# Outputs of paired chunks written channel-major by 64x32 tiles, in a fused gated linear attention and cosine-gated MLP on one core

## The chip, the core and the metric

The kernel runs on 1 core of one Trainium2 chip. The metric is the device time of one execution in microseconds. A run of before takes 192.56 us in the median of 13 (191.68 to 193.63).

## The reference

Inputs are q, k, v and f_logit of shape (4 batches, 8 heads, 768 steps, 48 channels) in float32, w_in (384 x 2048) and w_out (2048 x 384).

```python
f = 1.0 / (1.0 + np.exp(-f_logit))
state = np.zeros((B, H, D, D))
for t in range(S):
    state = f[:, :, t, :, None] * state + np.einsum('bhd,bhe->bhde', k[:, :, t], v[:, :, t])
    y[:, :, t] = np.einsum('bhd,bhde->bhe', q[:, :, t], state)
x = y.transpose(0, 2, 1, 3).reshape(B * S, H * D)
h = x @ w_in
out = (h * np.cos(h)) @ w_out
```

So there is a linear attention with a decay per channel, and then a two-layer network ("moe" in the code) over 3072 tokens with h cos h between the layers.

## The kernel before

The sequence is cut into chunks of 128 steps, 24 in all (6 per batch). Within a chunk the recurrence becomes matrix products: q times the cumulated decay b, k divided by it (bi), scores k q, a causal mask, and masked scores times v; what came before the chunk enters as q times the state. The first 12 chunks are handled as six **pairs** (`attend2`), the other 12 as **single** chunks (`attend`). A pair puts neighbouring time steps into one SBUF partition, so chunk x of the pair (x = 0, 1) lies in rows 64x to 64x+63, with an index e (or t in the loops) for even and odd steps.

The steps of a pair, by the lines of the profile:

- loads of k, q, v, f_logit by SP (L446; L438 for single chunks, and L426 for the weights);
- decay: exponential and logarithm on ScalarE (L484, L496), cumulated sums on TensorE (L507 to L513; L516 and L519 for single chunks), two exponentials out of PSUM (L524) into `b` and `bi`;
- products q b and k bi into `qk` on GpSimd or VectorE (L585; L679 for single chunks), cast of v into `vb` (L590, recorded at L432);
- transposes of `qk` on TensorE (L604) and their copy `qkt` (L606, recorded at L460; late single chunks use a DMA transpose, L692);
- scores on 64x64 tiles of TensorE (L617), mask `am` on VectorE (L623);
- the chunks' contribution to the state (`ps`, L637), then `move_state`: `st` = ps + state on VectorE (L542), `sz` = st times decay on GpSimd, in two halves (L549; a batch's first on VectorE), one after the other for the two chunks;
- the output `y` (function `pey`): state part L657, 96 moving columns for a pair of heads, and attention part L664, 64x128 tiles with 48 moving columns; it comes out with time in the partitions;
- `finish`: copy to `yb` in bf16 (L561), three transposes per chunk (`trx`, L568), and the copy to `xT` with channels in the partitions (L571); all copies are recorded at L460.

A single chunk's output (`pex`, L752) is already channel-major: the stationary operand is a slice of 32 channels of v (or of the state), the moving one the 128 columns of masked scores (or of transposed q), on tiles of 128 rows and 32 columns, four side by side. A 32-channel slice crosses from one head of 48 channels to the next in one slice of three; for these a second operand `vz` holds the 16 channels of each head beside zeros (L685, its four buffers are cleared at L378).

The network: `h` (L776) multiplies three 128-row parts of `xT` by w_in, cosine on ScalarE (L783), product `gT` on VectorE (L786), `o` (L798) multiplies 16 parts by w_out, copy `ot`, store by SP (L807, L810). It runs in units of 128, 128 and then 256 tokens, and its matmuls fill TensorE between the steps of the attention.

No order is written by hand. A planner (`Plan.run`) places every step on an engine by estimated costs: among the steps that could start within WINDOW ns of the earliest it takes the one with the lowest priority number. The table `PR` gives priorities (by kind of step: at, dec, f, h, k, o, tq, v, weights and gates for the switch of ScalarE's tables), `PIN` ties single steps to an engine. PSUM is one set of eight banks, from which every step takes one or two. `FORM` is the planner's cost of a change of TensorE's tile form. What the planner makes of it is a fixed order on each engine; each engine then runs its list in that order and waits at its head.

Of the kernel before, what the change touches and what calls it, by code (L numbers as in the profile page):

```python
# [116 lines left out]
class Plan:  # L117
# [6 lines left out]
    WINDOW = 200.0  # L124
# [128 lines left out]
def apart(tc, o, base):  # L253
# [13 lines left out]
    if banks and len(others) == len(banks):  # L267
        for b in banks:
# [11 lines left out]
    "at": [10.34, 1.66, 15.33, 9.78, -55.16, -54.85, -53.46, -27.65, -51, -51.02, -29.98, -1.78, 9.47,  # L280
          -24.05, -17.51, 26.44, 19.26, 41.61, 64.33, 60.95, 72.47, 41.29, 57.83, 70.66],
    "dec": [-40.13, -18.23, -118.54, -46.76, -113.79, -51.74],
    "f": [-33.54, 19.93, -13.27, 40.85, 11.69, 33.17, 10.24, 7.48, 19.13, 35.33, 34.56, -8.91, 83.83, 25.67,
          43.19, 50.91, 46.16, 41.23, 43.7, 50.92, 53.89, 87.57, 91.31, 90.43],
    "h": [9.97, 25.95, -30.53, 3.01, 6.76, -14.75, 87.35, 2.76, 40.79, 71.4, 37.51, 78.01, 62.23],
    "k": [-19.36, -9.86, -11.55, -8.7, 12.98, 15.54, 17.61, 50.25, 24.91, 19.36, 19.87, 27.13, 50.07, 53.19,
          47.56, 36.04, 66.28, 20.81, 59.57, 55.65, 83.79, 62.58, 85.61, 102.11],
    "o": [6.66, -5.11, 50.87, 98.39, 32.17, 119.14, -26.88, 103.85, 90.57, 149.42, 116.19, 123.67, 209.71],
    "tq": [29.88, 23.18, 15.76, 18.41, 3.3, 16.21, -23.62, 32.95, 98.96, 101.92, 58.74, 71.6, 53.32, 59.07,
          54.45, 42.26, 37.42, 40.36, 46.15, 7.47, 36.37, 39.29, 24.36, 18.36],  # L290
    "v": [-13.3, 8.45, -11.68, 3.43, 13.02, 15.37, 13.49, 28.89, 25.51, 21.76, 19.22, 48.22, 37.19, 43.36,
          51.52, 29.6, 40.85, 47.99, 28.14, 17.21, 52.36, 64.87, 53.96, 38.6],
    "w_in": [-7.72, -4.28, -1.16, -0.96],
    "w_out": [9.87, 4.13, 4.15, 9.92],
    "wc": [-56.67, -4.8, -15.98, -36.98, -13.35, -114.12, -134.73, -136.33],
    "gate": [None, 8, 3, 13, 20, 23],
}
PIN = {1: "DVE", 3: "ACT", 5: "POOL", 7: "POOL", 9: "POOL", 11: "DVE", 13: "POOL", 34: "DVE", 37: "POOL", 43:
       "DVE", 53: "DVE", 55: "DVE", 71: "DVE", 85: "DVE", 106: "DVE", 107: "POOL", 108: "POOL", 110: "DVE", 125:
       "ACT", 127: "DVE", 130: "DVE", 151: "ACT", 169: "POOL", 170: "POOL", 173: "ACT", 175: "ACT", 179: "DVE",  # L300
       187: "ACT", 189: "DVE", 213: "ACT", 219: "DVE", 231: "DVE", 232: "DVE", 234: "POOL", 235: "DVE", 253:
       "ACT", 277: "DVE", 295: "DVE", 297: "POOL", 298: "POOL", 301: "DVE", 305: "DVE", 319: "ACT", 342: "ACT",
       348: "DVE", 362: "DVE", 363: "DVE", 364: "POOL", 370: "DVE", 378: "DVE", 425: "POOL", 434: "ACT", 440:
       "POOL", 441: "ACT", 450: "DVE", 477: "DVE", 492: "POOL", 493: "ACT", 502: "DVE", 508: "POOL", 539: "ACT",
       545: "DVE", 560: "POOL", 561: "POOL", 576: "POOL", 577: "ACT", 582: "ACT", 603: "DVE", 624: "ACT", 633:
       "ACT", 639: "ACT", 640: "ACT", 670: "ACT", 691: "POOL", 692: "ACT", 701: "DVE", 707: "POOL", 717: "DVE",
       738: "DVE", 769: "DVE", 775: "POOL", 778: "ACT", 782: "ACT", 809: "ACT", 815: "ACT"}


def build(nc, cpool, ppool, q, k, v, f_logit, moe_w_in, moe_w_out, out):  # L310
    B, H, S, D = 4, 8, 768, 48
    C = 128
# [35 lines left out]
    def slots(name, n, shape, dt=BF16, zero=None):  # L348
        aps = [tl(shape, dt, f"{name}_{i}") for i in range(n)]
        if zero is not None and nc is not None:  # L350
            for t in aps:
                zero(t)
        return Slots(aps, name)
# [22 lines left out]
    vbB = halves("vb", 3, HD, BF16)  # L376
    vbS, vb2S = Banks(vbB, 1, [5, 4, 3, 2, 1, 0], "vb"), Banks(vbB, 2, [0, 2, 4], "vb2")
    vzS = slots("vz", 4, [128, NP, 96], zero=lambda t: nc.gpsimd.memset(t, 0.0))  # L378
# [4 lines left out]
    ybS = slots("yb", 2, [128, d_model])  # L383
# [14 lines left out]
    HB = lambda a: a.rearrange("p (h d) -> p h d", d=D)  # L398
# [159 lines left out]
    def finish(n, y, ycut, prio):  # L558

        yb, x = Val(ybS), xT[n]  # L560
        P.op("yb", {"ACT": act(384), "DVE": dve(384)}, lambda e: cp(e, yb.ap, ycut()),  # L561
             reads=[y], writes=[yb], prio=prio)
        px = Val(p1S)
        pxv = lambda: px.ap[:, 0:KM * C // 2].bitcast(BF16).rearrange("p (a n) -> p a n", n=C)

        def trx(e):
            for m in range(KM):
                nc.tensor.transpose(out=pxv()[:, m, :], in_=yb.ap[:, m * 128:(m + 1) * 128],  # L568
                                    identity=ident)
        P.op("trx", {"PE": mm(128, 3)}, trx, reads=[yb], writes=[px], prio=prio)  # L570
        P.op("xe", {"DVE": dve(384, 0.52), "ACT": act(384)}, lambda e: cp(e, x.ap, pxv()),  # L571
             reads=[px], writes=[x], prio=prio)

    E = lambda e: nc.vector if e == "DVE" else nc.gpsimd

    def attend2(b, c, n, ld, bt, bi, prio):
# [6 lines left out]
        for i in range(2):  # L583
            for j, (src, dec) in enumerate(((qf, bt), (kf, bi))):
# [5 lines left out]
        P.op("vb", {"POOL": 1050.0, "ACT": act(768, "S"), "DVE": 900.0}, lambda e: cast(e, vb.ap, vf.ap),  # L590
             reads=[vf], writes=[vb], prio=prio)
        twin = lambda j, p, e: qkv()[:, j, e, 2 * p:2 * p + 2, :].rearrange("p h d -> p (h d)")
        vv = lambda: vb.ap.rearrange("p (h e d) -> p e h d", e=2, d=D)
# [58 lines left out]
        py = Val(scS)  # L652

        def pey(e):
            for x in range(2):
                for p in range(NP if S[x] is not None else 0):
                    nc.tensor.matmul(py.ap[:, 512 * x + 96 * p:512 * x + 96 * p + 96],  # L657
                                     lhsT=qkts[p // 2].ap[:, 2 * x + p % 2, :],
                                     rhs=S[x].ap[:, p].rearrange("p t n -> p (t n)"), start=(p == 0), stop=False)
            for h in range(H):  # L660
                for t in range(2):
                    for x in range(2):
                        o = 512 * x + h * D
                        nc.tensor.matmul(py.ap[:, o:o + D],  # L664
                                         lhsT=ams[h // 4].ap[rows[x], h % 2, h % 4 // 2 * 2 + t, :],
                                         rhs=vv()[rows[x], t, h, :],
                                         start=(S[x] is None and h == 0 and t == 0), stop=(h == H - 1 and t == 1))
        P.op("y", {"PE": 845.0 if S[0] is not None else 680.0}, pey,
             reads=ams + [vb] + qkts + [x for x in S if x is not None], writes=[py], prio=prio,
             form=("full", "64x128"))  # L670
        for x in range(2):
            finish(n + x, py, lambda x=x: py.ap[:, 512 * x:512 * x + d_model], prio)

    def attend(b, c, n, ld, bt, bi, i, prio):
# [3 lines left out]
        for j, (src, dec) in enumerate(((qf, bt), (kf, bi))):  # L678
# [3 lines left out]
        vz = Val(vzS)  # L682
        P.op("vb", {"POOL": 530.0, "ACT": act(384, "S")}, lambda e: cast(e, vb.ap, vf.ap),
             reads=[vf], writes=[vb], prio=prio)
        P.op("vz", {"POOL": 270.0, "ACT": act(128, "S")}, lambda e: cast(  # L685
            e, vz.ap.rearrange("p s (r d) -> p s r d", d=48)[:, :, :, 0:16], vf.ap.rearrange(
                "p (s j d) -> p s j d", s=NP, d=16)[:, :, 2:4, :]), reads=[vf], writes=[vz], prio=prio)
# [34 lines left out]
        if c < NCH - 1:  # L722
            ps = Val(p1S)

            def pes(e):
                for p in range(NP):
                    nc.tensor.matmul(ps.ap[:, p * 2 * D:(p + 1) * 2 * D], lhsT=pair(1, p),  # L727
                                     rhs=vb.ap[:, p * 2 * D:(p + 1) * 2 * D],
                                     start=(p == 0), stop=(p == NP - 1))
            P.op("ps", {"PE": mm(96, 4)}, pes,  # L730
                 reads=[qk, vb] + ([S_in] if S_in is not None else []), writes=[ps], prio=prio)
            move_state(b, c, (ps, bt), lambda: ps.ap[:, 0:HD].rearrange("p (a t n) -> p a t n", t=2, n=D),
                       lambda: bt.ap[:, i, HD:], prio)
# [3 lines left out]
        def pex(e):  # L737
            ws, head = [], lambda h: am.ap[:, h % 2, h // 2, :]
            if S_in is not None:
                ws = [(t, S_in.ap[:, t // 3].rearrange("p t n -> p (t n)")[:, t % 3 * 32:t % 3 * 32 + 32],  # L740
                       qkt.ap[:, t // 3, :]) for t in range(12)]
            for r in range(2):
                for t in range(12):
                    s, k = t // 3, t % 3
                    if k == 1:
                        ws.append((t, vz.ap[:, s, 32 * r:32 * r + 32], head(2 * s + r)))
                    elif r == 0:
                        ws.append((t, vb.ap[:, 32 * t:32 * t + 32], head(2 * s + k // 2)))
            seen = set()
            for i, (t, w, m) in enumerate(ws):  # L750
# [5 lines left out]
             reads=[am, vb, vz, qkt] + ([S_in] if S_in is not None else []), writes=[px], prio=prio,  # L756
# [148 lines left out]
```

## Time and profile before

| | |
|---|---|
| median of 13 runs | 192.56 us |
| profiled execution, its own time | 192.56 us |
| its span, first to last instruction | 190.8 us |
| TensorE busy | 176.2 us, 92% |
| VectorE busy | 131.5 us, 69% |
| ScalarE busy | 127.0 us, 67% |
| GpSimd busy | 70.6 us, 37% |
| moe matmuls, L776 and L798 | 67.9 and 67.9 us |
| output of pairs, L657, L664 and L568 | 3.0, 3.7 and 4.0 us |
| output of single chunks, L752 | 4.7 + 4.1 + 3.5 us |

Busy times are of one execution. [...]the busy time of a group is longer than what it takes from TensorE; what it takes is read in the timeline, from the start of one group to the start of the next. In a row of instructions stand the line, the engine and operation, what is written and read, the shapes, and then the time and what ended the idle time before.

### The profile page before, as it was taken

To read this page: it belongs to the slowest core of one execution; us is meant where nothing else is said; L and a number is where in the kernel's file an instruction comes from. 1 tells how busy PE (TensorE), PEld (TensorE's weight loads), DVE (VectorE), ACT (ScalarE), POOL (GpSimd) and SP (SyncE) were. 2 spreads that over 40 slices of the span, in tenths; PEclk is the share of its full clock that TensorE was granted. 3 is DMA by queue.
4 is the path that set the end of the run, shared out by engine and by line. 5 is a ranking of instruction groups with operands and counts; after the bars stand their busy time and mean duration, and the time that the engine had idled before them with its cause. 6 is when DMAs were issued, how large, how long until landed. Compare 5 with 4: busy or idle time off the path is not lost.

```text
span 190.8 us, 5431 instructions
## 1 busy us (share of the span) xinstructions
PE 176.2 (92%) x2276; PEld 131.4 (69%) x2276; DVE 131.5 (69%) x169; ACT 127.0 (67%) x162; POOL 70.6 (37%) x109
## 2 busy tenths in 40 slices
PE   0688998999999999997799999999999999999993
PEld 0556897666788766686675668866778768876562
DVE  5478889859797929885798167996388895981100
ACT  5553867995488997797679947799955515861121
POOL 8544276043621113436932577205960240000000
PEclk9999999999999999999999999999999999999999
DMA  5999999989899998987999989973591101011122
GB/s 151 266 266 381 383 372 318 243 218 245 211 236 235 220 200 168 206 179 162 227 184 158 228 190 204 189 166 52 145 81 34 45 3 41 0 44 74 50 86 84
DMA packets 94121, 33.13 MB, mean 174 GB/s; under 512 B 87312, under 2 KB 92560, under 8 KB 94096
## 3 DMA queue, kind: packets, MB, share of 16 engines
q1 hardware_dynamic: 94096, 32.78, 74.1%
q8 instruction: 18, 0.29, 0.6%
q14 instruction: 7, 0.06, 0.1%
HBM read 25.17 MB, written 4.72 MB: 157 GB/s over the span
## 4 chain that ended last, share of the span: by engine, by line
PE 70%; DMA 8%; DVE 5%; issue 5%; POOL 5%; ACT 4%; SPq 3%; POOLq 0%; DVEq 0%; ACTq 0%
PE ps L798 30%; PE ps L776 26%; DMA ld<-in_q_dram 8%; PE ps L752 2%; PE ps L604 2%; PE ps L714 2%; SPq L446 2%; POOL sz L549 1%; DVE qk L585 1%; DVE am L623 1%; DVE gT L786 1%; ACT bi L524 1%; POOL qk L585 1%; PE ps L727 1%; POOL w_in_bf L432 1%
## 5 line engine op out<-in xcount | busy, mean ns | idle before, releaser
L776 PE MATMUL ps<-xT,w_in_bf 128*128 128x256 bf16 (+1 forms) x624 | 67.9, 265 | 0.5 <-DVE gT L786 0.5
L798 PE MATMUL ps<-w_out_bf,gT 128*128 128x384 bf16 (+2 forms) x400 | 67.9, 320 | 0.4 <-DVE xT L460 0.4
L783 ACT ACTIVATE cosh<-ps,halfpi 128x1024 bf16<-128x1024 f32 x48 | 53.0, 1113 | 20.0 <-PE ps L776 19.6
L786 DVE TENSOR_TENSOR gT<-ps,cosh 128x1024 bf16<-128x1024 f32 x48 | 57.9, 1221 | 10.3 <-ACT cosh L783 9.0
L776 PEld LDWEIGHTS <-w_in_bf 128*128 128x128 bf16 x624 | 56.1, 98 | 8.4 <-issue 0.8
L798 PEld LDWEIGHTS <-gT 128*128 128x128 bf16 x400 | 36.6, 98 | 21.7 <-issue 0.4
L549 POOL TENSOR_TENSOR sz<-st,b 64x192 bf16<-64x192 f32 x32 | 16.6, 519 | 31.9 <-DVE st L542 29.0
L717 DVE TENSOR_TENSOR am<-ps,umask 128x1024 bf16<-128x1024 f32 x12 | 14.5, 1217 | 6.7 <-ACT bi L524 3.7
L460 DVE COPY ot<-ps 128x384 f32<-128x384 f32 x12 | 6.6, 553 | 16.6 <-PE ps L798 16.6
L460 ACT COPY ot<-ps 128x384 f32<-128x384 f32 (+2 forms) x13 | 5.8, 455 | 16.4 <-PE ps L798 16.3
L623 DVE TENSOR_TENSOR am<-ps,pmask 128x1024 bf16<-128x1024 f32 x12 | 14.4, 1220 | 2.3 <-PE ps L617 2.2
L679 POOL TENSOR_TENSOR qk<-ld,b 128x384 bf16<-128x384 f32 x12 | 12.0, 1002 | 9.9 <-PE ps L798 5.5
L484 ACT ACTIVATE f<-f 128x768 f32<-128x768 f32 (+1 forms) x14 | 10.5, 747 | 4.8 <-DMA f<-in_f_logit_dram 4.8
L432 POOL CAST vb<-ld 128x384 bf16<-128x384 f32 (+1 forms) x13 | 7.8, 603 | 13.5 <-DMA ld<-in_v_dram 10.1
L524 ACT ACTIVATE b<-ps 128x776 f32<-128x776 f32 (+1 forms) x14 | 10.1, 722 | 3.1 <-PE ps L513 1.8
L679 POOL TENSOR_TENSOR qk<-ld,bi 128x384 bf16<-128x384 f32 x12 | 11.9, 998 | 0.0
L496 ACT ACTIVATE sp<-f 128x768 bf16<-128x768 f32 (+1 forms) x14 | 10.5, 752 | 0.4
L604 PE MATMUL ps<-ident,qk 128*128 128x128 bf16 x96 | 8.7, 250 | 1.8 <-POOL qk L585 1.1
L524 ACT ACTIVATE bi<-ps 128x768 f32<-128x768 f32 (+1 forms) x14 | 10.0, 717 | 0.0
L507 PE MATMUL ps<-sp,incl 128*128 128x384 bf16 x12 | 4.5, 378 | 5.4 <-ACT sp L496 5.3
L585 POOL TENSOR_TENSOR qk<-ld,b 128x384 bf16<-128x384 f32 x4 | 4.9, 1233 | 12.3 <-ACT b L524 10.6
L542 DVE TENSOR_TENSOR st<-ps,sz 128x384 f32<-128x384 f32 x16 | 8.8, 551 | 0.3 <-issue 0.2
(78 smaller groups left out, 189.4 us busy)
## 6 DMA issues: line engine op xcount, KB each, us to landing
f<-in_f_logit_dram SPq DMA_DIRECT2D x16, 192.0 KB, 4.2
ld<-in_k_dram SPq DMA_DIRECT2D x16, 192.0 KB, 3.8
ld<-in_q_dram SPq DMA_DIRECT2D x16, 192.0 KB, 3.9
gT<-in_moe_w_in_dram SPq DMA_DIRECT2D x4, 768.0 KB, 8.8
gT<-in_moe_w_out_dram SPq DMA_DIRECT2D x4, 768.0 KB, 11.7
ld<-in_v_dram SPq DMA_DIRECT2D x6, 384.0 KB, 5.4
out_dram<-ot SPq DMA_DIRECT2D x24, 96.0 KB, 2.6
ld<-in_v_dram SPq DMA_DIRECT2D x12, 192.0 KB, 3.6
```

Of the source, the lines that this page charges most:

```text
L460: (nc.scalar.copy if e == "ACT" else nc.vector.tensor_copy)(out=o, in_=i_)
L484: first = P.op("exp", {"ACT": act(384 * w, "S")}, lambda e, s=s: nc.scalar.activation(out=flat(ft.ap[:, s]), in_=flat(ft.ap[:, s]), func=A ...
L524: nc.scalar.activation(out=out_.ap[:, s, :], in_=pc.ap.rearrange("p (m n) -> p m n", m=w)[:, :, 0:n], func=AF.Exp, scale=sign)
L549: eng().tensor_mul(out=like(S_out.ap, pv())[s, ..., r, :], in0=srcap()[s, ..., r, :], in1=d[..., None].broadcast_to(list(d.shape) + [D]))
L604: nc.tensor.transpose(out=o[:, j, :, p, x, :], in_=twin(j, 2 * i + p, x), identity=ident)
L623: P.op("am", {"DVE": dve(1024)}, lambda e, sc=sc, am=am: nc.vector.tensor_mul(out=am.ap.rearrange("p r a n -> p (r a n)").rearrange("p (a ...
L679: P.op("qk", {"POOL": 1020.0}, lambda e, j=j, src=src, dec=dec: E(e).tensor_mul(out=qkv()[:, j, :, 0:D], in0=HB(src.ap), in1=HB(dec.ap[:, ...
L717: P.op("am", {"DVE": dve(1024)}, lambda e: nc.vector.tensor_mul(out=am.ap.rearrange("p r a n -> p (r a) n"), in0=sc.ap.rearrange("p (a n) ...
L776: nc.tensor.matmul(ph.ap[:, g * T:(g + 1) * T], lhsT=w_in_bf[:, f0 // 512, m, f0 % 512:f0 % 512 + 128], rhs=x[:, m, :], start=(g % (G // 2 ...
L783: nc.scalar.activation(out=co.ap, in_=ph.ap, func=AF.Sin, bias=halfpi),
L786: P.op("g", {"DVE": dve(1024)}, lambda e, ph=ph, co=co, gv=gv: nc.vector.tensor_mul(out=gv.ap, in0=ph.ap.rearrange("p (g t) -> p g t", t=T ...
L798: nc.tensor.matmul(po.ap[:, 0:z - a], lhsT=gT.ap[:, j, i * C:(i + 1) * C], rhs=w_out_bf[:, j, a:z], start=(j == 0), stop=(j == KF - 1))
```

## The change

`attend2` now writes its outputs channel-major as `attend` does. The matmuls of `y` are issued in two steps, one for each half of the heads (i = 0, 1), each as soon as that half's masked scores exist. The state part uses tiles of 128 rows and 32 columns, the attention part tiles of 64 rows (the chunk x) and 32 columns; both chunks' results go to one PSUM bank each, and one copy to `xT` follows. `yb`, `trx` and `finish` are gone.

`vb` is padded to 64 columns a head, with zeros in the last 16, so that a slice of 32 channels that crosses heads is read as two overlapping windows of it; `vz` goes, in single chunks too. `vb` of a pair is written with e outermost. The planner's WINDOW goes from 200 to 120, and nearly every entry of `PR` and `PIN` has another value, so the order of all engines is another.

```diff
-    WINDOW = 200.0
+    WINDOW = 120.0
...
-    vbB = halves("vb", 3, HD, BF16)
+    vbB = halves("vb", 3, H * 64, BF16, zero=lambda t: nc.gpsimd.memset(
+        t.rearrange("p (a d) -> p a d", d=64)[:, :, D:64], 0.0))
-    vzS = slots("vz", 4, [128, NP, 96], zero=lambda t: nc.gpsimd.memset(t, 0.0))
-    ybS = slots("yb", 2, [128, d_model])
...
-        py = Val(scS)
-
-        def pey(e):
-            for x in range(2):
-                for p in range(NP if S[x] is not None else 0):
-                    nc.tensor.matmul(py.ap[:, 512 * x + 96 * p:512 * x + 96 * p + 96], ...
...
-        P.op("y", {"PE": 845.0 if S[0] is not None else 680.0}, pey,
+        pxs, seen = [Val(p1S), Val(p1S)], set()
+        for i in range(2):
+            def pey(e, i=i):
+                ws, last = [], {}
+                for x in range(2):
+                    if S[x] is not None:
+                        ws += [(x, t, columns(S[x], t), qkts[i].ap[:, 2 * x + t // 3 % 2, :])
+                               for t in range(6 * i, 6 * i + 6)]
+                for e in range(2):
+                    for k in range(2):
+                        for t in range(6 * i, 6 * i + 6):
+                            for h, w in slices(t)[k:k + 1]:
+                                ws += [(x, t, vb.ap[rows[x], 512 * e + w:512 * e + w + 32],
+                                        ams[i].ap[rows[x], h % 2, h % 4 // 2 * 2 + e, :]) for x in range(2)]
...
+                for m, (x, t, w, a) in enumerate(ws):
+                    j = t % 4
+                    nc.tensor.matmul(pxs[x].ap[32 * j:32 * j + 32, t // 4 * C:t // 4 * C + C], lhsT=w, rhs=a,
+                                     start=(x, j) not in seen, stop=(i == 1 and last[x, j] == m))
+                    seen.add((x, j))
+            k = sum(x is not None for x in S)
+            P.op("y", {"PE": 225.0 + (96.0 if k else 0.0) + 88.0 * k}, pey,
...
+                 form=("128x32" if k else "64x32", "64x32"))
         for x in range(2):
-            finish(n + x, py, lambda x=x: py.ap[:, 512 * x:512 * x + d_model], prio)
+            P.op("xe", {"DVE": dve(384), "ACT": act(384)}, lambda e, x=x: cp(
+                e, xT[n + x].ap, pxs[x].ap[:, 0:HD].rearrange("p (a n) -> p a n", n=C)),
+                reads=[pxs[x]], writes=[xT[n + x]], prio=prio)
+
+    def slices(t):
+
+        s, k = t // 3, t % 3
+        return [(2 * s + k // 2, 128 * s + 40 * k)] if k != 1 else [
+            (2 * s, 128 * s + 32), (2 * s + 1, 128 * s + 48)]
```

In the tables, for example, the priorities of v:

```diff
-    "v": [-13.3, 8.45, -11.68, 3.43, 13.02, 15.37, ...
+    "v": [-13.48, 17.98, -0.36, -1.26, 5.93, -16.14, ...
```

## The prediction

> **What bounds the kernel now.** I read the page first, then the program's order of instructions before and after (which tells what stands behind what on every queue), then TensorE's timeline where the changed step runs, and last the waits that stop TensorE.
>
> ```profile
> PE 176.2 (92%) x2276; PEld 131.4 (69%) x2276; DVE 131.5 (69%) x169; ACT 127.0 (67%) x162; POOL 70.6 (37%) x109
> PE   0688998999999999997799999999999999999993
> DMA  5999999989899998987999989973591101011122
> PE 70%; DMA 8%; DVE 5%; issue 5%; POOL 5%; ACT 4%; SPq 3%; POOLq 0%; DVEq 0%; ACTq 0%
> ```
>
> TensorE is busy in 92% of the span and is 70% of the chain that ended last. Its idle slices are the head and two places near 85 to 90 us. VectorE, ScalarE and GpSimd have room on the average, so work taken from them pays only where TensorE waits for it. DMA is full up to about 125 us: a better order of loads can help, more speed of an engine cannot hasten them.
>
> To see what TensorE could save I laid its instructions end to end at the paces of its own timeline: 56 ns for 128 moving columns (8 transposes in 0.46 us at 49.70), 0.109 us for 256 (24 in 2.62 us), 0.162 us for 384 (8 in 1.30 us), and 0.10 us for each change of tile form. That gives about 167 us of work. The rest of the 190.8 us span is some 13.7 us up to the first moe matmul (20.41 us less 6.7 us of such work: the inputs, the chain of the first pair, and matmuls that run at half pace at first), some 7 us of waits after it, and 3.1 us behind the last matmul.
>
> **The pair's output step, before.**
>
> ```profile
> 80.31 0.50 PE L657 MATMUL ps<-sz,qkt 128*128 128x96 bf16 x8
> 80.74 0.57 PE L664 MATMUL ps<-vb,am 64*128 64x48 bf16 x32
> 81.25 0.62 PE L604 MATMUL ps<-ident,qk 128*128 128x128 bf16 x8
> 81.97 0.33 PE L568 MATMUL ps<-ident,yb 128*128 128x128 bf16 x3
> 82.14 0.33 PE L516 MATMUL ps<-sp,umask 128*128 128x384 bf16 x1
> ...
> 111.07 0.35 PE L752 MATMUL ps<-qkt,sz 128*32 128x128 bf16 x12
> 111.25 0.22 PE L752 MATMUL ps<-am,vb 128*32 128x128 bf16 x1
> ...
> 111.58 0.66 PE L798 MATMUL ps<-w_out_bf,gT 128*128 128x384 bf16 x3
> ```
>
> The first column is the start: TensorE is occupied from one start to the next. State part and attention part take 0.94 us (80.31 to 81.25), three transposes 0.17 us, twice a pair: 1.27 us. Where only one chunk has a state behind it (pairs 0 and 3) 4 of the 8 state matmuls fall out: 1.10 us. The lower rows are the single chunks' step, already of the new kind: 12 matmuls on four column tiles in 0.18 us, so three rounds of four at 56 to 60 ns, all four columns at work at once.
>
> **The same step after.** Per half of the heads: 12 matmuls of 128x32 (6 with one state), then 32 of 64x32. The new code sends the first along columns 0,1,2,3,0,1,0,1,2,3,0,1; [...]a column takes one at a time, so column 0, used four times, makes four rounds of 56 ns (two with one state). The second run, in each of its two passes, goes 0,1,2,3,0,1,1,0 in both row halves: columns 0 and 1 come three times, six rounds in all, 334 ns, though 32 matmuls on eight tiles could fit in four rounds. A half is 10 rounds, 0.56 us, a pair 1.11 us; with changes of form (in, between, and out, five for the pair) at 0.10 us it is 1.6 us, against 1.27 us with the transposes that go. For one state: 16 rounds 0.89 + 0.5 = 1.4 us against 1.1 us. That is 4 x 0.34 + 2 x 0.29 = +1.9 us. In the new order other steps stand together more often: changes of form over the whole kernel rise from 79 to 92 by the two orders, 13 and not the 18 that six pairs alone add, so 0.5 us comes off. **TensorE's work: +1.4 us.** The change makes the bound engine's work longer.
>
> [...] The row is above: column tiles with all 128 rows start together, 12 in 0.18 us. [...]I price by columns and rows; eight tiles at once, though, no row shows. [...] The row puts 0.10 us on it (the 32 small matmuls above, 16 pairs at 25 ns in 0.51 us from start to start, leave that), and I charge it 13 times.
>
> Bounds of the unknown: a 64x32 matmul costs 10.4 ns on average by my six rounds, 7 ns if the array packs better (-1.3 us over 384), 14 ns if eight tiles run at the pace of four, as at 111.07 (+1.4 us). I take 10.4, from the same timeline's rule that a busy column waits.
>
> **What is taken off the other engines.** Twelve yb copies (8 on ScalarE at 478 ns, 4 on VectorE at 557: 6.1 us); twelve vz casts (7 x 304 + 5 x 293: 3.6 us); four vz memsets at 412 ns, against three vb memsets near the 338 ns of the like row. The xT copies of pairs become f32: VectorE 552 in place of 353 ns, +0.2 us each. Pair vb casts write strided: between 824 ns (flat) and 1168 (the strided product) on GpSimd. None of this is on the path by itself; TensorE hides it except at three places.
>
> **Place 1, the head.**
>
> ```profile
> 16.35 1.09 PE L568 MATMUL ps<-ident,yb 128*128 128x128 bf16 x6 [0.57 <-ACT yb L460]
> 17.24 1.91 PE L604 MATMUL ps<-ident,qk 128*128 128x128 bf16 x16
> 20.41 1.04 PE L776 MATMUL ps<-xT,w_in_bf 128*128 128x128 bf16 x12
> ```
>
> Before, TensorE waits for yb and for its second copy (at half pace: six transposes take 0.9 us). These go. I followed the new order through with the old durations: the first q/k products are moved (k of half 0 to GpSimd, q of both halves to VectorE, where the second waits for its load at 7.45), which brings the second transposes to 8.65, 0.2 us earlier; the first qkt copies move to ScalarE (1.0 in place of 0.69 us) and hold up the second decay, so its last exponential ends at 16.1 instead of 15.2; the masks end at 14.4 instead of 13.9; the output's second half runs 15.0 to 16.05; the next transposes 16.05 to 18.1 instead of 17.24 to 19.1; the scores end at 19.5, the first moe matmul follows. The weights are no hindrance: v of the second pair now stands behind the first two w_in loads on SP's queue, and w_in lands 1.5 us earlier than its 17.0. So 20.41 becomes about 19.5 with 6.7 us of work before it in both: **-0.9 us**, and I add 0.2 us for the last w_in, cast at once by VectorE (26.8 before). Ends: -0.2 if the half-pace stretch lasts as long[...].
>
> **Places 2 and 3, near 90 us.**
>
> ```profile
> 89.05 0.33 PE L657 MATMUL ps<-sz,qkt 128*128 128x96 bf16 x4 [0.99 <-POOL sz L549]
> 91.10 0.34 PE L568 MATMUL ps<-ident,yb 128*128 128x128 bf16 x3 [0.25 <-DVE yb L460]
> 92.92 0.34 PE L727 MATMUL ps<-vb,qk 128*128 128x96 bf16 x4 [0.82 <-POOL qk L679]
> ```
>
> The waits for yb (0.4 us here, 0.2 at 57.4) have no successor: the xT copy reads the result itself. The wait for sz: in the new order 30 instead of 24 moe matmuls stand between the pair's state step and its output, 0.65 us more cover; but GpSimd does four qk products of 1.0 us ahead of that sz, and both halves of the output now stand behind it. I count half, -0.6. The third wait came from a q that SP issued at 86.03 and that landed at 90.3; in the new order the k and q of the first two single chunks stand some 25 us earlier in SP's queue and their products ahead of that sz, so -0.9. **Sum -2.1 us.** Other waits (some 3 us in small pieces, 0.45 at 138.6 behind the table load) I leave as they are: with every priority replaced some will go and some will come.
>
> **Sum.** +1.4 - 1.1 - 2.1 = -1.8 us on the profiled 190.8 us span, 189.0 us. That execution's own time is 192.56 us, 1.8 us around the span, and equals the median of the runs shown; so 190.7 us. Runs spread over 1%; a difference of 0.3%, 0.6 us, is about the least that a measurement can tell from none.
>
> **The rivals.** (a) The waits only change places: the gains near 90 us come back elsewhere, since TensorE stands behind sz chains in every pair. Then +1.4 - 1.1 - 0.6 (yb) = -0.3, 192.3 us, and a little worse order makes it slower; for it speaks that all queues are rearranged, against it the third wait's load, which is plainly earlier. (b) The eight tiles don't run at once: the place is the 64x32 run of each half, 384 matmuls; from 15 ns each (10.4 + 1.8 us / 384) the gain is used up; at 28 ns, two at a time, the time is 190.7 + 6.8 = 197.5 us. Against it the 64x64 rows, where four tiles in both directions share 32 matmuls in 0.57 us; for it that nothing here shows more than four. (c) The denser head reaches full pace sooner: 1.4 us more gained, 189.3. (d) The change doesn't earn it: order tables, pins and window are replaced too, so a gain may be the rearranged loads' alone; by my sum it is, but for the yb waits and the head's.
>
> **How the numbers follow.** Forecast 0.50, (c) 0.18, (a) 0.22, (b) 0.10. Of (a) 0.06 is faster, 0.08 the same, 0.08 slower; of the forecast 0.46 is faster, 0.04 the same; (b) is slower. Faster 0.70, same 0.12, slower 0.18. The range takes (c) with the better packing, -1.4 - 1.3, down to 188.0, and (a) with the 14 ns price, up to 193.7; most of (b) is left out.
>
> **What would show it.** Right: y of a half taking about 0.75 us from start to start with six steps of 56 ns in its 64x32 run; first moe matmul near 19.5; no matmul waiting for a q near 90 us; TensorE's matmuls up from 2276 to 2512 while its idle time falls by some 3 us. Wrong: 64x32 matmuls 14 ns or more apart; idle time before the output's first matmuls, by sz or am; a first moe matmul after 20.4.

## The result, and the profile after

The changed kernel takes 191.06 us in the median of 11 runs, before 192.95 in 48 runs taken beside it: ratio 0.989, 95% interval 0.9864 to 0.9917. Two of the 11 runs took 194.3 and 194.4 us, at a granted clock of 0.99, and are left out of the ratio. The profiled execution took 191.32 us with a span of 189.5, against 192.56 and 190.8.

From the page of after:

```profile
PE 176.6 (93%) x2512; PEld 131.5 (69%) x2512; DVE 131.2 (69%) x161; ACT 125.7 (66%) x152; POOL 68.0 (36%) x102
PE   0689979999999999999999999999899999999993
...
DMA  5999999999999859989899997989610900102022
PE 81%; DVE 6%; issue 3%; DMA 3%; ACT 3%; SPq 2%; POOL 1%; DVEq 0%; POOLq 0%; ACTq 0%
```

TensorE has 236 matmuls more and hardly more busy time. The two sevens near 90 us in its row are nines now, and the chain that ended last is TensorE for 81% instead of 70%, with DMA down from 8% to 3%. The DMA row is full up to about 125 us before and 130 us after, and the bytes are the same, so the loads were put in another order, not made fewer. New in TensorE's row is the seven in the sixth slice, near 26 us.

The pair's output step, in TensorE's timeline of after (start, time, engine, line, operands, how many):

```profile
80.75 0.40 PE L653 MATMUL ps<-qkt,sz 128*32 128x128 bf16 x12
81.08 0.52 PE L653 MATMUL ps<-am,vb 64*32 64x128 bf16 x32
81.52 0.42 PE L600 MATMUL ps<-qkt 48*64 48x128 bf16 x16
...
85.03 3.45 PE L768 MATMUL ps<-xT,w_in_bf 128*128 128x256 bf16 x30
88.40 0.40 PE L653 MATMUL ps<-qkt,sz 128*32 128x128 bf16 x12
88.73 0.52 PE L653 MATMUL ps<-am,vb 64*32 64x128 bf16 x32
89.18 0.40 PE L653 MATMUL ps<-qkt,sz 128*32 128x128 bf16 x12
89.51 0.52 PE L653 MATMUL ps<-am,vb 64*32 64x128 bf16 x32
89.96 1.26 PE L768 MATMUL ps<-xT,w_in_bf 128*128 128x256 bf16 x10
```

Read the starts: 0.33 us for the state part (busy for 0.40), 0.45 for the attention part, 0.77 us for a half. No row carries a bracket with a wait, where before waited for sz, yb and a single chunk's product. The same stretch in the table by windows (width, then busy us of PE, PEld, DVE, ACT, POOL, granted clock, DMA share, GB/s); first before, then after:

```profile
84.00:96.00 12.00, 9.94 (x136) 8.14 (x135) 8.20 (x11) 8.91 (x12) 9.20 (x11) 1.00 0.94 189
```

```profile
84.00:96.00 12.00, 12.00 (x215) 10.21 (x212) 7.96 (x9) 10.40 (x12) 4.04 (x7) 1.00 0.94 185
```

The head of after:

```profile
15.24 0.40 PE L653 MATMUL ps<-qkt,sz 128*32 128x128 bf16 x6
15.57 0.83 PE L653 MATMUL ps<-am,vb 64*32 64x128 bf16 x32
16.33 1.78 PE L587 MATMUL ps<-ident,qk 128*128 128x128 bf16 x16
18.45 0.42 PE L600 MATMUL ps<-qkt 48*64 48x128 bf16 x16 [0.35 <-DVE qkt L458]
...
19.40 1.31 PE L768 MATMUL ps<-xT,w_in_bf 128*128 128x128 bf16 x15
```

The first moe matmul starts at 19.40 us, 1.0 us earlier than before. And a place that was not foreseen, the second pair's output:

```profile
24.21 0.40 PE L653 MATMUL ps<-qkt,sz 128*32 128x128 bf16 x12
24.55 0.35 PE L653 MATMUL ps<-am,vb 64*32 64x128 bf16 x14
26.29 0.40 PE L653 MATMUL ps<-am,vb 64*32 64x128 bf16 x18 [1.40 <-issue]
```

In the middle of one run of 32 matmuls, with all operands there, TensorE stands still: its last start is at 24.68 us, the next at 26.29. "issue" means that it waited for nothing that the profile shows.

To find where the time went, I laid TensorE's instructions end to end at the paces of the prediction and took what each start lay behind that as lost (my sums from the two traces; the terms leave some 0.15 us of each span over):

| us | before | after | difference |
|---|---|---|---|
| TensorE's work, end to end | 166.7 | 168.4 | +1.7 |
| lost up to 24 us | 14.3 | 13.4 | -0.9 |
| lost 24 to 30 us | 0.2 | 1.65 | +1.45 |
| lost 30 to 84 us | 2.6 | 1.75 | -0.8 |
| lost 84 to 96 us | 2.65 | 0.04 | -2.6 |
| lost behind 96 us | 1.05 | 1.2 | +0.2 |
| behind the last matmul | 3.15 | 2.9 | -0.25 |
| span | 190.8 | 189.5 | -1.3 |

### The profile page after: what moved, and what is told of

Same layout as the page of the kernel before. It is cut to its first block, busy times and chain, and to the rows that moved or that the text cites. A ratio compares the mean times of both kernels' runs of the same rounds, so it can differ in the third digit from the quotient of the medians.

```text
span 189.5 us, 5879 instructions
## 1 busy us (share of the span) xinstructions
PE 176.6 (93%) x2512; PEld 131.5 (69%) x2512; DVE 131.2 (69%) x161; ACT 125.7 (66%) x152; POOL 68.0 (36%) x102
## 4 chain that ended last, share of the span: by engine, by line
PE 81%; DVE 6%; issue 3%; DMA 3%; ACT 3%; SPq 2%; POOL 1%; DVEq 0%; POOLq 0%; ACTq 0%
PE ps L768 33%; PE ps L790 30%; PE ps L653 5%; DMA ld<-in_v_dram 3%; PE ps L744 3%; DVE qk L567 3%; PE ps L711 2%; PE ps L600 2%; SPq L444 2%; PE ps L587 2%; DVE am L606 2%; ACT bi L522 1%; PE ps L620 1%; PE ps L514 1%; DVE qkt L458 1%
## 5 line engine op out<-in xcount | busy, mean ns | idle before, releaser
L775 ACT ACTIVATE cosh<-ps,halfpi 128x1024 bf16<-128x1024 f32 x48 | 53.3, 1113 | 25.0 <-PE ps L768 24.3
L790 PE MATMUL ps<-w_out_bf,gT 128*128 128x384 bf16 (+2 forms) x400 | 69.0, 320 | 0.0
L768 PE MATMUL ps<-xT,w_in_bf 128*128 128x256 bf16 (+1 forms) x624 | 66.2, 264 | 0.2
L790 PEld LDWEIGHTS <-gT 128*128 128x128 bf16 x400 | 36.0, 98 | 21.4
L458 DVE COPY ot<-ps 128x384 f32<-128x384 f32 x14 | 7.7, 553 | 13.5 <-PE ps L790 13.4
L680 POOL TENSOR_TENSOR qk<-ld,b 128x384 bf16<-128x384 f32 x12 | 12.0, 998 | 11.2 <-DMA ld<-in_q_dram 5.2
L606 DVE TENSOR_TENSOR am<-ps,pmask 128x1024 bf16<-128x1024 f32 x12 | 14.3, 1219 | 1.7 <-PE ps L600 1.7
L714 DVE TENSOR_TENSOR am<-ps,umask 128x1024 bf16<-128x1024 f32 x12 | 14.3, 1217 | 0.4 <-PE ps L711 0.4
L458 ACT COPY ot<-ps 128x384 f32<-128x384 f32 (+2 forms) x11 | 5.0, 454 | 13.5 <-PE ps L790 11.9
L430 POOL CAST vb<-ld 128x384 bf16<-128x384 f32 (+1 forms) x11 | 6.8, 621 | 15.0 <-DMA ld<-in_v_dram 5.8
L458 ACT CAST xT<-ps 128x384 bf16<-128x384 f32 x13 | 6.0, 483 | 9.2 <-PE ps L744 6.3
L567 POOL TENSOR_TENSOR qk<-ld,b 128x384 bf16<-128x384 f32 x5 | 6.0, 1198 | 16.9 <-ACT b L522 16.9
L482 ACT ACTIVATE f<-f 128x768 f32<-128x768 f32 (+1 forms) x14 | 10.4, 744 | 1.4 <-DMA f<-in_f_logit_dram 1.3
```

Of the source, the lines that this page charges most:

```text
L458: (nc.scalar.copy if e == "ACT" else nc.vector.tensor_copy)(out=o, in_=i_)
L567: P.op("qk", {"POOL": 1150.0, "DVE": 800.0}, lambda e, j=j, i=i, src=src, dec=dec: E(e).tensor_mul(out=parts[j][i].ap.rearrange("p e h d - ...
L606: P.op("am", {"DVE": dve(1024)}, lambda e, sc=sc, am=am: nc.vector.tensor_mul(out=am.ap.rearrange("p r a n -> p (r a n)").rearrange("p (a ...
L680: P.op("qk", {"POOL": 1020.0}, lambda e, j=j, src=src, dec=dec: E(e).tensor_mul(out=qkv()[:, j, :, 0:D], in0=HB(src.ap), in1=HB(dec.ap[:, ...
L714: P.op("am", {"DVE": dve(1024)}, lambda e: nc.vector.tensor_mul(out=am.ap.rearrange("p r a n -> p (r a) n"), in0=sc.ap.rearrange("p (a n) ...
L768: nc.tensor.matmul(ph.ap[:, g * T:(g + 1) * T], lhsT=w_in_bf[:, f0 // 512, m, f0 % 512:f0 % 512 + 128], rhs=x[:, m, :], start=(g % (G // 2 ...
```

## Experiments

Every kernel below was timed in five rounds against before on the same chip; ratios are to before, with 95% intervals. "Work" and "lost" are the sums of the table above. Added lines shift line numbers.

**1. The changed kernel again**, no edit, for its trace.

> The changed kernel once more, unedited, for a ratio on the same chip as the three kernels beside it and for a second trace. Theory: 0.990 of before (191 us), and in the trace the first moe matmul at 19.4 us and about 0.6 us less head, 2.5 us less waits near 90 us. In the first trace TensorE stands still for 1.6 us within the attention part of the second pair's second half (24.7 to 26.3 us) with nothing shown to wait for; a block of instructions of 16 KB is fetched from 23.6 to 24.7 us, just before. If the fetch is the cause the stop is there again at the same instruction; if it was chance of that one execution, it is gone or elsewhere.

0.989 [0.9848, 0.9931], span 189.6. The stop came again, 1.73 us, before the same instruction: the 701st of TensorE's weight loads and matmuls, both counted. It is a property of the program, not of one execution.

**2. The new code with the tables of before.**

```diff
-    WINDOW = 120.0
+    WINDOW = 200.0
```

with PR as before, and each pin of before on the step of the same name (not shown).

> The new output step and padded v with the priorities, pins and window of before (pins carried over step by step; those of steps that no longer exist fall out). Theory of the prediction: the step itself makes TensorE's work longer, and the gain near 90 us is the new order's. TensorE's work by the paces is 169.3 us here, 2.5 us over before; less 0.6 us of waits for the copy yb and up to 0.9 us in the head: 193.5 to 195 us, ratio 1.003 to 1.01. Rival, the step itself brings the gain (shorter chain, work off the other engines): ratio 0.985 to 0.995.

1.0417 [1.0379, 1.0455], far off what was expected. The tables don't carry an order over: the planner made another one from them, with lost time in many places (work 169.3, lost 25.9 us). It shows only how much hangs on tables that fit their steps.

**3. The pair's output in one step**, all twelve slices behind both masks, with unchanged tables (the pins numbered anew for the steps).

```diff
-        for i in range(2):
-            def pey(e, i=i):
-...
-                        for t in range(6 * i, 6 * i + 6):
+        def pey(e):
+...
+                    for t in range(12):
```

> The output of a pair in one step for all heads instead of two halves: 24 state matmuls in six rounds over the four columns, 64 attention matmuls in eight rounds (each column is used equally often), where the halves need 8 and 12 rounds. Theory (the columns of one half are unevenly used, TensorE is the bound): TensorE's work 165.4 us against 168.4 of the changed kernel, 3.0 us less, of which up to 1 us is lost again in the head since the first output waits for the second mask: 188 to 189.5 us, ratio to before 0.975 to 0.985. Rival (the time is set by the waits, and halves were made to start early): no gain over the changed kernel, ratio 0.99 or above.

1.0638 [1.0573, 1.0703]. In the profiled execution (207.49 us, granted clock 0.959) work falls to 165.4 us, but 37.0 are lost, some 16 of them between 120 and 150 us, far from the step. Again the planner's order broke, so this says nothing on the step. From here on, orders were held fixed.

**4. The same order on all engines, but the two row halves in turn**: all slices of chunk x = 0, then all of x = 1, so that no two neighbours can use the two row halves of a column.

```diff
-                for e in range(2):
-                    for k in range(2):
-                        for t in range(6 * i, 6 * i + 6):
-                            for h, w in slices(t)[k:k + 1]:
-                                ws += [... for x in range(2)]
+                for x in range(2):
+                    for e in range(2):
+                        for k in range(2):
+                            for t in range(6 * i, 6 * i + 6):
+                                for h, w in slices(t)[k:k + 1]:
+                                    ws += [(x, ...)]
```

> The changed kernel with the attention matmuls of a half sent in another sequence: first all of chunk x = 0, then all of x = 1, so that the two row halves of the array do not work side by side. Nothing else moves. If eight tiles really work at once and TensorE is the bound, each half takes some 0.28 us longer, 3.4 us over twelve halves: ratio to before 1.005 to 1.01, to the changed kernel 1.015 to 1.018. If weight loads, not the tiles, set the pace of the 64x32 run, or waits set the time, the two sequences take the same: 0.990.

The timeline of this kernel:

```profile
82.48 0.40 PE L654 MATMUL ps<-qkt,sz 128*32 128x128 bf16 x12
82.81 0.64 PE L654 MATMUL ps<-am,vb 64*32 64x128 bf16 x32
83.38 0.42 PE L600 MATMUL ps<-qkt 48*64 48x128 bf16 x16
```

The same 32 matmuls take 0.57 us from start to start, against 0.45 in after. So in after the row halves do run side by side. The ratio is 0.9937 [0.9909, 0.9964]: a higher midpoint than after's, by less than expected. A half costs 0.13 us more and not 0.28, that is 1.5 us over twelve halves instead of 3.4. The rest of this trace changes too, and about cancels: the stop at 26 us is gone (1.6 us less); a stop that ends at 53.95 us takes 1.19 us, where after has one of 0.64 us before the same instruction (see the last section); and 128-column matmuls still start 107 ns apart up to 22.4 us, in after up to 17.7, which costs some 1.1 us.

**5 and 6. All TensorE instructions shifted by 104 places**: 52 matmuls of one moving column into an unused PSUM column, in the first pair's cumulated sums; run twice.

```diff
+                    extra = lambda m: [nc.tensor.matmul(o[:, 511:512], lhsT=incl, rhs=incl[:, 0:1], start=True,
+                                                        stop=True) for _ in range(m if chunks[0][2] == 0 else 0)]
                     if dual:
+                        if i == 0:
+                            extra(24)
...
+                        if i == 1:
+                            extra(28)
                         return
```

> The changed kernel with 52 matmuls of one column each, on operands that are ready, put into TensorE's first idle stretches (24 ahead of the first cumulated sum, 28 behind the second); their result lands in unused columns. That is 104 more instructions ahead of everything, so the blocks of TensorE's instructions end elsewhere. Theory (the stop of 1.6 to 1.7 us in the second pair's output is TensorE out of instructions, since the small tiles use two instructions in 9 ns): the block that was fetched from 23.6 us is fetched before the output begins, the stop is gone or under 0.4 us, and the time falls by 1.2 to 1.7 us: ratio to before 0.981 to 0.984. Rival (the stop is a wait on data that the trace doesn't name): it stays at the same instruction, ratio 0.988 to 0.991.

> The kernel after with 52 matmuls of one moving column added in the first pair's cumulated sums, so that all later TensorE instructions stand 104 places further in its program; a second time, for more runs. Theory (the stop of 1.6 us in the second pair's second half is TensorE waiting for its next block of instructions, whose place in the program is shifted): the stop is absent again and the ratio to before is 0.978 to 0.987. Rival (the stop was hidden from the end by waits that come later): 0.986 to 0.992, as the kernel after.

The second pair's output, first execution:

```profile
24.12 0.40 PE L659 MATMUL ps<-qkt,sz 128*32 128x128 bf16 x12
24.45 0.52 PE L659 MATMUL ps<-am,vb 64*32 64x128 bf16 x32
24.90 2.83 PE L774 MATMUL ps<-xT,w_in_bf 128*128 128x128 bf16 x36
```

The stop is gone, in both. The ratios are 0.9878 [0.9822, 0.9933] and 0.9853 [0.9801, 0.9905]. Both midpoints lie under after's 0.989, but the intervals overlap it, so what the stop costs at the end isn't settled by six runs each: from nothing to about 1%. The traces show why it needn't come through. The first execution has a span of 187.5 us, the second 189.0, and the second loses 1.9 us near 135 us, behind a product of GpSimd and a DMA transpose, where the first loses none.

**7. The halves of pairs 1, 3 and 5 joined** where nothing stands between them on TensorE, order otherwise as it is. 64 matmuls in one run use the four columns evenly: fewer rounds, fewer changes of form.

```diff
+            a.joined = a.name == o.name == "y" and o in a.after
+...
+                both = i == 1 and ys[0].joined
+                ts = range(12) if both else range(6 * i, 6 * i + 6)
```

> The changed kernel in its own order of steps, but where the two halves of a pair's output follow each other on TensorE (pairs 1, 3 and 5) they are sent as one run over all twelve slices, in which every column is used equally often. Nothing else moves. Theory (uneven columns cost two rounds of four in the state part and four of twelve in the attention part, and TensorE is the bound): 0.5 us less in each of the three, 1.5 us in all, ratio to before 0.981 to 0.984; the stop in the second pair may grow, since the run uses instructions faster still, then 0.985. Rival (waits set the time): ratio 0.988 to 0.991.

0.9925 [0.99, 0.995]: no gain over after. Work did fall, from 168.4 to 166.9 us; lost rose from 18.1 to 21.1. Three rows of its timeline hold about half of the rise; in after the stop is 1.40 us and the wait for GpSimd's qk 0.53 us, once:

```profile
26.94 0.34 PE L656 MATMUL ps<-am,vb 64*32 64x128 bf16 x18 [1.70 <-issue]
...
136.40 0.40 PE L701 MATMUL ps<-ident,qk 128*128 128x128 bf16 x4 [0.95 <-POOL qk L683]
137.35 0.40 PE L701 MATMUL ps<-ident,qk 128*128 128x128 bf16 x4 [0.56 <-POOL qk L683]
```

**8. Joined and shifted.**

> The kernel after with the halves of pairs 1, 3 and 5 joined to one run of 64 matmuls that uses the four columns evenly (TensorE's work 1.5 us less), and with the 52 one-column matmuls of the shift. Theory (the joined form was held up by the stop of 1.9 us and by a late q): without the stop some 1.5 us less than the joined form alone, ratio to before 0.980 to 0.987, the best so far. Rival (the joined form waits for the second half's scores and for later loads, and gives its saving back whatever the stop does): 0.987 to 0.993.

0.9825 [0.977, 0.9879], the lowest ratio of all, inside what the theory expected; the interval overlaps that of after. The median over all its six runs is 191.0 us (188.94 to 193.75), as after's. The profiled execution, 193.75 us, is the slowest of the six and tells little of the others. So this is a candidate, not a shown improvement on the changed kernel.

**9 and 10. The new output step in the order of before**, on every engine: before's plan is left as it is, the new matmuls stand where the old ones did, the copy yb writes xT at once, and the transposes, their copies and the vz casts issue nothing. In 9 the matmuls come by halves, in 10 all twelve slices together.

```diff
-        P.op("trx", {"PE": mm(128, 3)}, trx, reads=[yb], writes=[px], prio=prio)
+        P.op("trx", {"PE": mm(128, 3)}, lambda e: None, reads=[yb], writes=[px], prio=prio)
...
-            for h in range(H):
-                for t in range(2):
-                    for x in range(2):
+            for ts in (range(6), range(6, 12)):
+                for e in range(2):
+                    for k in range(2):
+                        for t in ts:
```

> The kernel before with its plan unchanged on every engine: only the contents of steps are exchanged. The pair's output is computed as in the change (the two halves one after the other in one step), the copy yb writes xT itself, transposes and second copy are empty, v is padded and the vz casts are empty. So this is the new step without the new order. By the prediction's sum: TensorE's work 169.0 us against 166.7, +2.3 us; less the waits for yb, 0.6 us in the middle and about 0.5 in the head: +1.0 us, ratio 1.003 to 1.008. Rival (the step alone brings the gain): 0.985 to 0.995.

> As the kernel beside it, with the pair's output sent over all twelve slices at once, so that each column is used equally often: TensorE's work 165.9 us against 166.7 of before. Theory (uneven columns are what the new step costs): -0.8 us of work and -1.1 us of waits for yb, ratio to before 0.988 to 0.993, 3 us under the kernel with halves. Rival (TensorE's work in this step doesn't reach the end): the two are equal.

By halves: 1.0136 [1.0084, 1.0188]. So in before's order the kernel with this step is slower. Work is 169.0 us (+2.3), and the stop is there, before the same 701st instruction:

```profile
24.04 0.45 PE L666 MATMUL ps<-am,vb 64*32 64x128 bf16 x26
26.52 0.28 PE L666 MATMUL ps<-am,vb 64*32 64x128 bf16 x6 [2.02 <-issue]
```

Soon behind it, from 28.0 to 31.2 us, 128-column matmuls start 107 ns apart again and not 56, which costs some 1.4 us. Whether the stop brings this on isn't shown; after has its stop and no such stretch. The two together, 3.6 us, are more than the 3.0 us by which this span (193.8 us) is longer than before's. So the run doesn't tell what the step costs without them.

All at once: work 165.9 us, 0.8 less than before, and yet 1.0123 [1.0073, 1.0173], where a gain was expected. The timeline shows the late products of before, grown:

```profile
94.57 0.34 PE L736 MATMUL ps<-vb,qk 128*128 128x96 bf16 x4 [1.35 <-POOL qk L690]
...
99.02 0.34 PE L736 MATMUL ps<-vb,qk 128*128 128x96 bf16 x4 [0.83 <-POOL qk L690]
```

With a wait of 1.3 us for VectorE's qk at 18.29 and the stop of 1.4 us at 26.30, lost is 23.8 us. Three us less work than by halves did not reach the end.

**11. The kernel before with six loads exchanged** in SP's queue, nothing else.

```diff
+        for a, b in (("v23", "q14"), ("v16", "k12"), ("v17", "q12")):
+            turn(order, a, b)
```

> The kernel before, with nothing changed but SP's order of six loads (and with it the buffers that they use): q of chunk 14, k of chunk 12 and q of chunk 12 take the places of v of chunks 23, 16 and 17, which are used 25 us and more later. Theory (the waits near 90 us come from loads that SP issues late; the change's gain is that they stand earlier in SP's queue): in the kernel before GpSimd waits 2.64 us at 82.4 for q of chunk 14 and 1.46 us at 89.0 for q of chunk 12; with these loads issued near 75 and 76 us instead of 80.5 and 85.4, both waits go, TensorE's waits of 0.99 us for sz (89.05) and 0.82 us for a single chunk's k (92.92) go with them, and nothing later takes them back: 0.99 + 0.82 = 1.8 us, ratio 0.989 to 0.992. This alone would be the change's gain. Rival (the waits only change places: the q comes in time, but TensorE meets the next late step behind it): ratio 0.996 to 1.001.

0.9995 [0.9975, 1.0016]: the rival's forecast holds. TensorE's timeline between 85 and 95 us, then GpSimd's:

```profile
87.77 0.50 PE L673 MATMUL ps<-sz,qkt 128*128 128x96 bf16 x8
...
93.31 0.34 PE L743 MATMUL ps<-vb,qk 128*128 128x96 bf16 x4 [2.21 <-POOL qk L695]
```

```profile
91.80 0.50 POOL L448 CAST vb<-ld 128x384 bf16<-128x384 f32 x1 [3.11 <-DMA ld<-in_v_dram]
```

The wait for sz at 89.05 is gone: its eight matmuls stand in one row, with no bracket. But GpSimd, no longer waiting for q, waits for the next load in its list, a v that SP issued at 87.17 and that landed at 91.68, and TensorE's third wait grows from 0.82 to 2.21 us.

**12. The same with that v moved forward**, and k of chunk 12 where it was.

```diff
-("v16", "k12")
+("v16", "v14")
```

> As the kernel with six loads exchanged, but with v of chunk 14 in the place of v of chunk 16, and k of chunk 12 where it was: there GpSimd, which no longer waited for q, waited 3.11 us for v of chunk 14 (landed at 91.68), and TensorE 2.21 us at 93.31 behind it. Theory (the waits near 90 us are those of loads that stand too late in SP's queue, and go when each of them stands early enough): v of chunk 14 is issued near 76 us instead of 87, k of chunk 12 lands near 89.6 as before, so GpSimd's next product ends near 90.6 and TensorE's wait of 2.21 us falls under 0.4 us; the ratio to before is 0.988 to 0.993. Rival (waits only change places: the next late load or another engine takes the time at a later place): TensorE's waits from 84 to 102 us still sum to over 1.5 us, or as much is lost behind 102 us, and the ratio is 0.996 to 1.002.

0.9975 [0.9956, 0.9993], a quarter of a per cent. TensorE and GpSimd once more:

```profile
91.48 0.34 PE L743 MATMUL ps<-vb,qk 128*128 128x96 bf16 x4
91.72 3.45 PE L792 MATMUL ps<-xT,w_in_bf 128*128 128x256 bf16 x30
96.99 0.34 PE L743 MATMUL ps<-vb,qk 128*128 128x96 bf16 x4 [1.82 <-POOL qk L695]
```

```profile
95.00 0.99 POOL L695 TENSOR_TENSOR qk<-ld,b 128x384 bf16<-128x384 f32 x1 [2.61 <-DMA ld<-in_q_dram]
```

The wait at 93.31 went and turned up at 96.99, behind q of chunk 13. In the changed kernel the k and q of chunks 12 and 13 are issued at 43.7, 44.4, 52.9 and 54.3 us; in before at 85.4, 86.0, 89.5 and 90.2. So one or two loads of this group weren't enough. Whether moving the whole group, and nothing else, would have been was not tried.

## Why the prediction came out as it did

Predicted were 1.8 us less, 190.7 from 192.56 or a ratio of 0.991. The ratio of 0.989 is 2.1 us less, and the two profiled spans differ by 1.3. The large terms were of the right kind and about the right size; that the sum fits this well is in part luck, as the fourth term shows.

**TensorE's work: +1.4 predicted, +1.7 by the same paces in the trace.** The step itself was right: 0.75 us a half was given, 0.77 is read off. Experiment 4 confirms the picture behind it. In the single starts of the trace, the first eight 64x32 matmuls of a run begin 3 to 4 ns apart, then come five gaps of 32 to 47 ns (8, 8, 4, 4, 4 and 4 starts), so six steps in all; the 32 take 10.4 ns each with one change of form of 0.11 us, where 0.10 was charged. That is the value taken between 7 and 14 ns. Rival (b), tiles that don't run at once, is refuted: it needed 15 ns. Where in the sum the other 0.3 us stands I haven't found.

**The head: -0.9 predicted, -1.0 measured** for the first moe matmul, which starts at 19.40 where 19.5 was forecast. The second output ends at 16.33 instead of 16.05, and what stands between it and the moe matmul takes 3.1 us instead of 3.45. Full pace did come sooner, as rival (c) has it; that the denser head brought it isn't shown. In the single starts of before, 128-column matmuls are 107 ns apart up to 20.7 us and 56 from 20.9; in after the change comes at 17.8 us, within the 16 transposes, and the first moe matmuls already run at 56. But it is worth much less than the 1.4 us of (c), itself an estimate: by mine 0.5 us, for 16 scores that take 0.35 us instead of 0.58 and five moe matmuls at 56 ns instead of 107. The first of these, 0.2 us, is part of the 1.0; in what the head lost in all, 0.9 us less, both are contained. So by this estimate the chain itself gained somewhat less than was forecast, and the pace made it up. The time of the change isn't the program's alone: in the two executions of experiments 5 and 6 it comes at 17.7 and at 16.7 us. What sets it isn't shown. The -0.2 that was forecast for the early cast of the last w_in can't be told apart: the wait of 0.5 us at 30.18 before, for a gate product, is gone, but it was not named.

**The waits near 57 and 90 us: -2.1 predicted; -2.6 between 84 and 96 us.** All three went, the one for sz wholly and not by half. Experiments 11 and 12 sharpen the reason. The prediction traced the third to one late q and counted on the k and q of two chunks coming earlier together. With single loads moved forward in before's order, each wait that went came back at the next late load, and of 1.8 us some 0.5 arrived. In the change the k and q of two chunks stand 36 to 42 us earlier, together (the prediction read some 25), and no wait came back here. That this group is what did it is the best reading of the traces, not shown by a run of its own.

**"Other waits I leave as they are".** This is the step that failed, with errors of both signs, together +0.85 us: -0.8 us between 30 and 84 us (though a second stop, of 0.6 us at 52.6, lies there), +0.2 behind 96, where the wait of 0.45 us at 138.6 went and this one came,

```profile
135.86 0.40 PE L698 MATMUL ps<-ident,qk 128*128 128x128 bf16 x4 [0.53 <-POOL qk L680]
```

and +1.45 us for the stop at 26.3, of which the prediction had nothing. It looked for what 32 small matmuls cost on the array and not for whether TensorE is fed fast enough for them.

**Rival (d), that the change doesn't earn it,** is not decided, but the runs lean to it. The new step in the old order did not gain: 1.4% and 1.2% slower (experiments 9 and 10), with the stop in both. With its own order, and the stop as well, the kernel is 1.1% faster than before, and most of the gain lies between 84 and 96 us, where the loads came in another order. What the step would do in the old order without the stop, and whether the old step with an order made for it would do as well, was not tried. **Rival (a), waits that only change places,** failed for the change as a whole but holds for nearly every single edit: experiments 7, 10, 11 and 12 each took away work or waits of 0.8 to 1.8 us, and at most 0.5 us of it reached the end. In experiment 10 the stop of 1.4 us has a part in that.

## What to carry to other kernels

A wait that the profile put down to a late load came back here at the next one (2.21 us at 93.31 in experiment 11, 1.82 us at 96.99 in 12): before crediting its removal, look what stands next in the waiting engine's list and when that lands. Where engines run fixed lists, compare an edit in the unchanged order on every engine before believing it; a re-planned order made the time here 4 and 6% longer than before's, and TensorE work saved in a step was seen at the end in no kernel where the intervals could tell it. When one step becomes many small matmuls, ask also whether the instructions come fast enough; by my reading of the traces they did not in after, at a loss of 1.6 and 0.64 us.

## What was not expected of the hardware

By my reading of the traces TensorE ran out of instructions here. In after it stands still for 1.6 us before the 701st of its weight loads and matmuls and for 0.64 us before the 1469th, and the profile names nothing that it waits for. The page of after lists the transfers of program code as their own queue:

```profile
q8 instruction: 19, 0.31, 0.7%
```

that is 16 KB each, taking 1.12 us in the mean (1.09 in before). I take them for TensorE's, since their number goes with its instructions: 18 in before, 19 in after and 20 in the shifted kernel, for 4552, 5024 and 5128 weight loads and matmuls. That is 253 to 264 for each transfer; my estimate is that one holds 256, for the two stops of after lie 768 apart and the transfers ahead of them are the second and the fifth. For these kernels the traces give the time of the second transfer and how many weight loads and matmuls TensorE had started at its start and end:

| kernel | transfer, us | started at its start and end | stop |
|---|---|---|---|
| before | 25.6 to 26.7 | 595, 629 | none |
| after | 23.6 to 24.7 | 583, 698 | 1.6 us before the 701st |
| after, again | 23.7 to 24.8 | 584, 700 | 1.7 us before the 701st |
| halves joined | 24.3 to 25.5 | 586, 700 | 1.9 us before the 701st |
| new step, old order, halves | 23.8 to 24.9 | 646, 700 | 2.2 us before the 701st |
| new step, old order, whole | 23.8 to 24.9 | 536, 700 | 1.4 us before the 701st |
| row halves in turn | 23.7 to 24.8 | 521, 560 | none |
| shifted | 19.7 to 20.8 | 555, 585 | none |

In a run of 64x32 tiles a matmul and its weight load take 10.4 ns, and in after TensorE started 115 instructions within this one transfer (583 to 698). The five executions with a stop have it at the same place, and go on 1.35 to 1.65 us after the transfer's end. The three without had started 629, 560 and 585 instructions at that end.

The same happens once more, 768 instructions further on. In after:

```profile
52.60 0.52 PE L600 MATMUL ps<-qkt 48*64 48x128 bf16 x22 [0.42 <-issue]
```

The row starts with the 1469th, and the fifth transfer ended at 51.14 us, 1.46 us earlier; from the start before it 0.64 us pass. After, again, has it too (0.62 us), and in the kernel with the row halves in turn this is the 1.19 us at 53.95, where the transfer ended at 52.60. In the shifted kernels neither stop is there.

So I went through all fourteen traces, that of before among them, at every 256th instruction: the 445th with the first transfer, the 701st with the second, and so on, 252 places. TensorE never starts one earlier than 1.35 us after the end of its transfer (the least is 1.47 in after, 2.49 in before). The instruction just ahead of such a place isn't held: the 700th starts up to 0.6 us before the transfer ends. So a block of instructions that comes too late is my reading of the stop, which no row of a trace names as its cause. The shift speaks for it: it changes little but the place (its 52 matmuls also fill some of the head), and both stops go. Why 1.35 us pass after the transfer is open.
